# Attention with mixed heads: v's products on 128 rows and half the columns of the array

## The chip, the cores and the metric

The kernel runs on one core of one Trainium2 chip. The metric is the device time of one execution in microseconds (us). The engines are TensorE (in the profile PE for matmuls, PEld for its weight loads), VectorE (DVE), ScalarE (ACT), GpSimd (POOL) and SyncE (SP, which here only issues transfers). Three timed runs of the kernel before gave 973.60, 975.28 and 977.43 us; the median is 975.28 us.

## The reference

Four batches, 12 heads, 448 positions, 64 numbers per head. The scores of all heads are mixed by a 12 x 12 matrix before the softmax, and its result by another one after it. What comes out goes through two dense layers with a leaky rectifier between them.

```python
scores = scale * np.matmul(q, k.transpose(0, 1, 3, 2))
scores = np.einsum('bhij,hg->bgij', scores, w_pre)
attn = np.exp(scores - np.max(scores, axis=-1, keepdims=True))
attn = attn / (np.sum(attn, axis=-1, keepdims=True) + 1e-09)
attn = np.einsum('bhij,hg->bgij', attn, w_post)
attn_out = np.matmul(attn, v)
x = attn_out.transpose(0, 2, 1, 3).reshape(B * S, H * D)      # 1792 x 768
h = x @ w_in                                                  # 768 x 2048
g = np.maximum(h, 0.0) + alpha * np.minimum(h, 0.0)
return g @ w_out                                              # 2048 x 768
```

The arrays w_in, w_out and alpha arrive as 64-bit floats and are rounded in the kernel.

## The kernel before, in words

The work has two phases. The first is the attention, the second the two dense layers (L430 to L530), which read the attention's output back from device memory (`x2`).

Phase one takes queries in 16 chunks: four per batch, with 120, 120, 120 and 97 queries (`CHUNKS`; the last one is used from its row 7 on, 90 queries). A chunk's scores are made head pair by head pair (`qk`, L146), copied by ScalarE to `st` (L154) and sent by DMA into another layout (`relay`, L163), in which 10 queries by 12 heads lie on the partitions. A group is ten queries; two groups make a block, and there are 90 blocks. For each block `mix` (L171) multiplies by w_pre, VectorE takes the row maximum (`rmax`, L176), ScalarE the exponential and its sum (`exp`, L183), VectorE scales w_post by the sums (`norm`, L189 to L193), and `post` (L205) multiplies by that, which also turns the block so that keys lie on the partitions. `post_out` (L215) copies the result into `at`, a tile of [128, 4, 12, 120]: the 448 keys are four blocks of 128, where the last one holds 64, in heads and queries.

`pv` (L217 to L235) multiplies `at` of a whole chunk by `v`, in two halves that stand in two neighbouring steps. Its output `x` takes two banks of PSUM, with three pairs of heads in each. Each product uses a quarter of TensorE's array, 64 rows by 64 columns: 64 keys of one head. Rows 0 to 63 hold the even blocks of 64 keys, rows 64 to 127 the odd ones; the two heads of a pair lie on the two column halves. While rows 0 to 63 add into one bank, rows 64 to 127 add into the other, and in the second half of `pv` the banks are exchanged (`bank = r ^ half`), so that in the end both banks have all keys. The last block of 64 odd keys does not exist, so the lower rows do 24 products of a half and the upper ones 18: 42 in all.

The program never lets both row halves add into one bank at one time: between the halves of `pv` VectorE copies one column of `at` onto itself (L401 to L405): the copy comes after the first half, which reads that tile, and the second half waits for it. `pv_out` (L237) copies both banks to `xe` after the second half.

`step(m)` (L381) writes out the order of the work by hand. On TensorE it is: `mix` of block m+1, `post` of block m-2, and then up to two places for other work, `(m, 0)` and `(m, 1)`; the table `places` puts a `qk` head pair or a half of `pv` into each. The first half of `pv` stands at the second place of a step, the second half at the first place of the next. VectorE also does the rounding of w_in and w_out in between (`convert`, L52 to L58), SP loads q, k, v and those weights, GpSimd issues the relays.

`v` comes from a pool of two buffers, a new tile for each batch (L131 to L134).

Of the kernel before, what the change touches and what calls it, by code (L numbers as in the profile page):

```python
# [8 lines left out]
F32 = mybir.dt.float32  # L9
# [10 lines left out]
B, H, S, D = 4, 12, 448, 64  # L20
DM, DFF = 768, 2048
# [7 lines left out]
CW = 120  # L29
# [3 lines left out]
NS = 4  # L33
NJ = S // 64
# [27 lines left out]
def talking_heads_prelu(ctx: ExitStack, tc: tile.TileContext, q, k, v, w_pre, w_post, mask, w_in, w_out, alpha, out):  # L62
    nc = tc.nc
# [23 lines left out]
    pool = lambda name, bufs, **kw: p1.enter_context(tc.tile_pool(name=name, bufs=bufs, **kw))  # L87
# [6 lines left out]
    sm = pool("sm", 4)  # L94
    ep = pool("ep", LAG + 2)
    rp = pool("rp", LAG + 1)
    vp = pool("vp", 2)
    ap_ = pool("ap", 2)
    xep = pool("xep", 2)
    ps_m = pool("ps_m", 2, space=PSUM)  # L100
# [6 lines left out]
    wq = mixw.tile([128, H, HI], F32, name="wq")  # L107
    NSR = 2 * (RAHEAD + 1)
    sr_b = [srp.tile([128, S], F32, tag=f"sr{i}", name=f"sr{i}") for i in range(NSR)]
    pa = ps_a.tile([128, 2, 512], F32, tag="a", name="pa")  # L110


    k_t, q_t, v_t, s_t, a_t = {}, {}, {}, {}, {}
# [14 lines left out]
                               in_=q[b, :, H * c0 + NP * hf * cn:H * c0 + NP * (hf + 1) * cn])  # L128

    def load_v(b, s):  # L130
        if s == 0:  # L131
            v_t[b] = vp.tile([128, NS, DM], F32, tag="v", name=f"v{b}")
        n = min(128, S - 128 * s)
        nc.sync.dma_start(out=v_t[b][:n, s, :], in_=v[b, 128 * s:128 * s + n])  # L134

# [29 lines left out]
    def mix(m):  # L165

        ps = ps_m.tile([128, 2, 512], F32, tag="m", name=f"m{m}")
        ga, gb = sr_t.pop(2 * m), sr_t.pop(2 * m + 1)
        for hf, g in ((0, ga), (64, gb)):
            for u, r in ((0, slice(0, 64)), (1, slice(64, SR0 + GP))):  # L170
                nc.tensor.matmul(ps[hf:hf + 64, u, :S], wk[r, :], g[r, :], start=True, stop=True)  # L171
        m_t[m] = ps

    def rmax(m):
        nm = sm.tile([128, 2], F32, tag="nm", name=f"nm{m}")
        nc.vector.tensor_reduce(out=nm, in_=m_t[m][:, :, :S], axis=AX.X, op=ALU.max, negate=True)  # L176
        nm_t[m] = nm
# [39 lines left out]
    def pv(ci, half):  # L217


        b, c = chunk_list[ci]  # L220
        cn = ROWS[c][1] * GI
        if half == 0:
            u_t["pv", ci] = ps_s.tile([128, 2, 512], F32, tag="s", name=f"x{ci}")
        ps = u_t["pv", ci]
        for cl in range(3):
            for s in range(NS):
                for r in range(2 if 2 * s + 1 < NJ else 1):
                    bank = r ^ half
                    pr = slice(64 * r, 64 * r + 64)
                    for t in range(2):  # L230
                        h = 2 * (3 * bank + cl) + t
                        nc.tensor.matmul(ps[64 * t:64 * t + 64, bank, cl * CW:cl * CW + cn],  # L232
                                         v_t[b][pr, s, h * D:(h + 1) * D], a_t[ci][pr, s, h, :cn],
                                         start=(half == 0 and s == 0 and cl == 0),
                                         stop=(half == 1 and 2 * s + 2 + r >= NJ and cl == 2))  # L235

    def pv_out(ci, half):  # L237

# [51 lines left out]
    places = {}  # L290
    for ci in range(NC):
        m = (first[ci + 1] - 1) // 2 + LAG + 1
# [21 lines left out]
    with tc.manual_schedule():  # L314
        p0 = ExitStack()
        start = p0.enter_context(tc.tile_pool(name="start", bufs=1))
# [20 lines left out]
        for t in sr_b:  # L337
            nc.vector.memset(t[:SR0], 0.0)
        nc.vector.memset(pa, 0.0)
        for i, w in enumerate((w_pre, w_post)):  # L340
            for p in ((SR0, 64), (0, 64))[i]:
                nc.gpsimd.dma_start(out=mask_sb[p:p + HP, i], in_=mask[:HP, :HI, :])
                nc.gpsimd.dma_start(out=wb[p:p + HP, i, :],
                                    in_=w.rearrange("(o h) g -> o h g", o=1).to_broadcast([HI, H, H]))
# [36 lines left out]
        def step(m):  # L381


            nonlocal done
            for f, *args in jobs.get(m, []):
                f(*args)
            if live(m + 1):
                mix(m + 1)
            now, later[:] = list(later), []
            for f in now:  # L390
                f()
            if live(m - LAG):
                post(m - LAG)
            if live(m - 1):
                norm(m - 1)
            if live(m + 1):
                rmax(m + 1)
            if live(m):
                exp(m, 0)
            use((m - 1, 1), 1)  # L400
            if places.get((m, 0), " ")[0] == "pv":  # L401


                col = a_t[places[m, 0][1]][:, :, :, 0]
                nc.vector.tensor_copy(col, col)  # L405
            if m >= 0:
                relays(2 * (m + 2 + RAHEAD) if m > 2 else first[1], (nc.gpsimd,))
            if live(m):
                exp(m, 1)
            use((m, 0), 0)  # L410
            if live(m - LAG):
                post_out(m - LAG)
            use((m, 0), 1)
            use((m, 1), 0)
            want = (m + 1) * conv_steps // (NB - 4)
            while done < want and done < conv_steps:
                next(conv, None)
                done += 1
# [95 lines left out]
        for u in range(NU + 1):  # L514
            b, f = divmod(u, NFC)
# [4 lines left out]
            if u < NU:  # L520
                split_w(u, 1)
                ps = l1(u)
# [44 lines left out]
```

## Time and profile before

| | |
|---|---|
| median of three runs | 975.28 us |
| the profiled execution | 971.61 us, of which the span of instructions is 969.8 us |
| TensorE matmul | 827.7 us busy (85%), 11540 instructions |
| TensorE weight load | 671.6 us (69%), 11540 instructions |
| VectorE | 488.0 us (50%), 870 instructions |
| ScalarE | 441.5 us (46%), 870 instructions |
| mean granted clock of TensorE | 0.963 of 2.4 GHz |

A written matmul on 32-bit floats appears as two matmul records and two weight loads. A row of the timeline merges neighbours of one kind: start, length from the first start to the last end, engine, line, operation, tiles, shape, number, and in brackets the idle time before them and what ended it. "issue" stands where the profile knows nothing that the engine waited for. `64*64` in a TensorE row is the used part of the array (rows by columns), `64x120` the moving operand. PEclk is the granted share of 2.4 GHz.

### The profile page before, as it was taken

The numbers are of one execution on the slowest core, as the hardware profiler recorded it, in microseconds if no ns is written. First come the engines' busy times: TensorE is split into PE (matmuls) and PEld (weight loads), VectorE is DVE, ScalarE is ACT, GpSimd is POOL, SyncE is SP. The second block draws the span as 40 slices with busy tenths as digits, with TensorE's granted clock in tenths as the row PEclk, the third lists the DMA queues.
The fourth block names the chain that finished last, engine by engine and source line by source line (L and its number), as shares of the span: only waits on it lengthen the run. The fifth ranks groups of instructions, "written<-read, shape, count | busy, mean of one in ns | idle before, by whom it ended". The sixth has DMA issues, their size and how long they took to land.

```text
span 969.8 us, 26257 instructions
## 1 busy us (share of the span) xinstructions
PE 827.7 (85%) x11540; PEld 671.6 (69%) x11540; DVE 488.0 (50%) x870; ACT 441.5 (46%) x870; POOL 353.7 (36%) x315
## 2 busy tenths in 40 slices
PE   6757767777777786787759999999999999999998
PEld 3335544444555453455649999999999999999997
DVE  3756666655766775678252246432454225532222
ACT  1756756665656785677422233333223223233222
POOL 2312222221222221222035545545545545545542
PEclk9989999998989999999879999999999999999999
DMA  6996798765887867775088000200002000010001
GB/s 166 245 255 190 207 267 214 207 186 186 230 248 209 244 207 217 216 217 172 20 305 337 1 10 10 95 1 1 18 2 95 1 1 20 1 57 1 1 1 57
DMA packets 55166, 124.03 MB, mean 128 GB/s; under 512 B 26028, under 2 KB 32988, under 8 KB 55052
## 3 DMA queue, kind: packets, MB, share of 16 engines
q1 hardware_dynamic: 39846, 81.71, 27.7%
q0 software_dynamic: 14208, 37.56, 14.1%
q10 hardware_dynamic: 998, 3.09, 1.0%
q8 instruction: 90, 1.47, 0.6%
q14 instruction: 24, 0.20, 0.1%
HBM read 59.96 MB, written 23.62 MB: 86 GB/s over the span
## 4 chain that ended last, share of the span: by engine, by line
PE 68%; issue 15%; ACT 6%; DMA 5%; POOL 3%; DVE 3%; ACTq 0%; SPq 0%; POOLq 0%; DVEq 0%
PE h L471 24%; PE acc L496 24%; PE x L232 6%; PE pa L205 5%; PE m L171 4%; PE s L146 4%; ACT at L215 3%; ACT st L154 3%; POOL sr L163 2%; DMA sr<-st 2%; DMA v<-in_v_dram 1%; DVE nm L176 1%; DMA xr<-x 1%; DMA wb<-in_w_post_dram 1%; ACT e L183 0%
## 5 line engine op out<-in xcount | busy, mean ns | idle before, releaser
L471 PE MATMUL h<-xs,wi 128*128 128x448 f32 x1152 | 246.4, 368 | 12.7 <-DVE xs L461 11.4
L496 PE MATMUL acc<-g,wo 128*128 128x448 f32 x1152 | 243.7, 365 | 0.0
L471 PEld LDWEIGHTS h<-xs,wi 128*128 128x128 f32 x1152 | 218.1, 189 | 30.7 <-issue 11.5
L163 POOL DMA_DIRECT2D sr<-st x174 | 107.0, 617 | 339.4 <-PE m L171 245.3
L496 PEld LDWEIGHTS acc<-g,wo 128*128 128x128 f32 x1152 | 216.4, 188 | 17.0
L449 POOL TENSOR_TENSOR wi<-wr,wi 128x768 fp32r<-128x768 f32 x64 | 118.6, 1854 | 256.5 <-ACT wi L448 256.5
L176 DVE TENSOR_REDUCE nm<-m 128x2 f32<-128x896 f32 x90 | 98.1, 1089 | 137.1 <-PE m L171 137.1
L480 DVE TENSOR_SCALAR t<-h,alpha_sb 128x448 f32<-128x448 f32 x64 | 43.8, 684 | 236.0 <-PE h L471 236.0
L482 ACT CAST g<-t 128x448 fp32r<-128x448 f32 x64 | 36.3, 567 | 271.3 <-DVE t L481 271.3
L205 PEld LDWEIGHTS pa<-r,e 64*64 64x64 f32 x5040 | 110.4, 139 | 71.0 <-issue 47.5
L146 PE MATMUL s<-k,q 64*64 64x448 f32 (+2 forms) x768 | 103.6, 594 | 55.3 <-ACT st L154 49.9
L205 PE MATMUL pa<-r,e 64*64 64x60 f32 x5040 | 111.5, 226 | 28.2 <-issue 24.1
L215 ACT COPY at<-pa 128x480 f32<-128x480 f32 x180 | 93.1, 572 | 81.6 <-PE pa L205 77.3
L449 POOL TENSOR_TENSOR wo<-wr,wo 128x768 fp32r<-128x768 f32 x64 | 125.2, 1956 | 5.4 <-ACT wo L448 5.4
L183 ACT ACTIVATE e<-m,nm 128x448 f32<-128x448 f32 x180 | 115.2, 646 | 5.4 <-DVE nm L176 3.5
L232 PE MATMUL x<-at,v 64*64 64x120 f32 (+1 forms) x2688 | 91.7, 275 | 26.0 <-issue 16.8
L171 PE MATMUL m<-sr,wk 64*64 64x448 f32 (+1 forms) x720 | 97.3, 575 | 14.8 <-issue 9.1
L154 ACT COPY st<-s 120x896 f32<-120x896 f32 (+1 forms) x93 | 84.9, 913 | 45.1 <-PE s L146 44.9
L232 PEld LDWEIGHTS x<-at,v 64*64 64x64 f32 x2688 | 82.7, 141 | 31.6 <-issue 18.5
L146 PEld LDWEIGHTS s<-k,q 64*64 64x64 f32 (+2 forms) x768 | 23.9, 134 | 98.3 <-ACT st L154 86.4
L448 ACT CAST wo<-wr 128x768 fp32r<-128x768 f32 x64 | 53.5, 836 | 57.2 <-PE acc L496 57.2
L483 DVE TENSOR_TENSOR g<-t,g 128x448 fp32r<-128x448 f32 x64 | 40.8, 638 | 44.6 <-ACT g L482 44.6
(40 smaller groups left out, 489.1 us busy)
## 6 DMA issues: line engine op xcount, KB each, us to landing
sr<-st POOLq DMA_DIRECT2D x174, 210.0 KB, 6.0
cr<-in_w_in_dram SPq DMA_DIRECT2D x16, 768.0 KB, 7.2
cr<-in_w_out_dram SPq DMA_DIRECT2D x16, 768.0 KB, 6.9
wsc<-ct SPq DMA_DIRECT2D x32, 384.0 KB, 6.4
wr<-wsc SPq DMA_DIRECT2D x14, 768.0 KB, 9.9
xr<-x SPq DMA_DIRECT2D x24, 224.0 KB, 3.8
out_dram<-o SPq DMA_DIRECT2D x24, 224.0 KB, 2.0
k<-in_k_dram SPq DMA_DIRECT2D x21, 224.0 KB, 5.9
```

The lines of the kernel that those rows point to most:

```text
L146: nc.tensor.matmul(ps[lo:hi, hf, :S], q_t[ci][r, p, lo:hi], k_t[b][r, p, :], start=True, stop=True)
L154: copy(dst[:cn, p], u_t.pop(("qk", ci, p))[:cn, :, :S])
L163: dma.dma_start(out=sr_t[n][SR0:SR0 + GP], in_=s_t[ci][r0:r0 + (GI - 1) * st + 1:st])
L171: nc.tensor.matmul(ps[hf:hf + 64, u, :S], wk[r, :], g[r, :], start=True, stop=True)
L176: nc.vector.tensor_reduce(out=nm, in_=m_t[m][:, :, :S], axis=AX.X, op=ALU.max, negate=True)
L183: nc.scalar.activation(out=e_t[m][:, u], in_=m_t[m][:, u, :S], func=AF.Exp, bias=nm_t[m][:, u:u + 1], scale=1.0, accum_out=se_t[m][:, u:u ...
L205: nc.tensor.matmul(dst[:, :, HI * u:HI * u + HI], e[h, u, 64 * jb:64 * jb + 64], r[h, u].rearrange("p (h i) -> p h i", h=H), start=True, s ...
L215: nc.scalar.copy(dst, pa[:, g, :NS * GP].rearrange("p (s i) -> p s i", i=GI))
L232: nc.tensor.matmul(ps[64 * t:64 * t + 64, bank, cl * CW:cl * CW + cn], v_t[b][pr, s, h * D:(h + 1) * D], a_t[ci][pr, s, h, :cn], start=(ha ...
L449: nc.gpsimd.tensor_tensor(t[:, 1], w, t[:, 0], ALU.subtract)
L471: nc.tensor.matmul(ps[:, :S], w[:, tw, cc * 128:(cc + 1) * 128], x[:, tx, cc, :], start=(i == 0), stop=(i == 3 * NCC - 1))
L496: nc.tensor.matmul(accs[c][:, :S], w[:, tw, c * 128:(c + 1) * 128], g[:, tg], start=(f == 0 and i == 0), stop=(f == NFC - 1 and i == 2))
```

## The change

`pv` now uses all 128 rows and half the columns for one product: 128 keys of one head. A half of `pv` does the three head pairs of one bank completely (24 products, the two heads of a pair on the two column halves) and the other half those of the other bank. No bank is exchanged, and the copy on VectorE between the halves is gone. Since the fourth block has only 64 keys, rows 64 to 127 of that block are filled with zeros: the two buffers of `v` are made once, with a name each, are zeroed there at the start, and the loads of v write the first 64 rows only.

```diff
@@ -94,7 +94,7 @@
     sm = pool("sm", 4)
     ep = pool("ep", LAG + 2)
     rp = pool("rp", LAG + 1)
-    vp = pool("vp", 2)
+    vp = pool("vp", 1)
     ap_ = pool("ap", 2)
     xep = pool("xep", 2)
     ps_m = pool("ps_m", 2, space=PSUM)
@@ -107,6 +107,7 @@
     wq = mixw.tile([128, H, HI], F32, name="wq")
     NSR = 2 * (RAHEAD + 1)
     sr_b = [srp.tile([128, S], F32, tag=f"sr{i}", name=f"sr{i}") for i in range(NSR)]
+    v_b = [vp.tile([128, NS, DM], F32, tag=f"v{i}", name=f"v{i}") for i in range(2)]
     pa = ps_a.tile([128, 2, 512], F32, tag="a", name="pa")
@@ -128,8 +129,7 @@
                                in_=q[b, :, H * c0 + NP * hf * cn:H * c0 + NP * (hf + 1) * cn])
     def load_v(b, s):
-        if s == 0:
-            v_t[b] = vp.tile([128, NS, DM], F32, tag="v", name=f"v{b}")
+        v_t[b] = v_b[b % 2]
         n = min(128, S - 128 * s)
         nc.sync.dma_start(out=v_t[b][:n, s, :], in_=v[b, 128 * s:128 * s + n])
@@ -224,15 +224,10 @@
         ps = u_t["pv", ci]
         for cl in range(3):
             for s in range(NS):
-                for r in range(2 if 2 * s + 1 < NJ else 1):
-                    bank = r ^ half
-                    pr = slice(64 * r, 64 * r + 64)
-                    for t in range(2):
-                        h = 2 * (3 * bank + cl) + t
-                        nc.tensor.matmul(ps[64 * t:64 * t + 64, bank, cl * CW:cl * CW + cn],
-                                         v_t[b][pr, s, h * D:(h + 1) * D], a_t[ci][pr, s, h, :cn],
-                                         start=(half == 0 and s == 0 and cl == 0),
-                                         stop=(half == 1 and 2 * s + 2 + r >= NJ and cl == 2))
+                for t in range(2):
+                    h = 2 * (3 * half + cl) + t
+                    nc.tensor.matmul(ps[64 * t:64 * t + 64, half, cl * CW:cl * CW + cn], v_t[b][:, s, h * D:(h + 1) * D],
+                                     a_t[ci][:, s, h, :cn], start=(s == 0), stop=(s == NS - 1))
     def pv_out(ci, half):
@@ -337,6 +332,8 @@
         for t in sr_b:
             nc.vector.memset(t[:SR0], 0.0)
         nc.vector.memset(pa, 0.0)
+        for t in v_b:
+            nc.vector.memset(t[S % 128:, NS - 1, :], 0.0)
         for i, w in enumerate((w_pre, w_post)):
             for p in ((SR0, 64), (0, 64))[i]:
                 nc.gpsimd.dma_start(out=mask_sb[p:p + HP, i], in_=mask[:HP, :HI, :])
@@ -398,11 +395,6 @@
             if live(m):
                 exp(m, 0)
             use((m - 1, 1), 1)
-            if places.get((m, 0), " ")[0] == "pv":
-                col = a_t[places[m, 0][1]][:, :, :, 0]
-                nc.vector.tensor_copy(col, col)
             if m >= 0:
                 relays(2 * (m + 2 + RAHEAD) if m > 2 else first[1], (nc.gpsimd,))
             if live(m):
```

On TensorE, the two steps in which the first chunk's `pv` stands, before. The names are those of the program with its running numbers; `m` is the output of `mix`, `pa` of `post`, `x` of `pv`. "x41" says that the row stands for 41 such instructions as written, and brackets name the engines or DMA queues that the instruction waits for.

```order
L205 MATMUL pa_118<-r6_669,e6_608 64x12x5 x27
L232 MATMUL x0_733<-at0_369,v0_252 64x120 [waits DMAHW1_49,PE_49]
L232 MATMUL x0_733<-at0_369,v0_252 64x120 x3
...
L232 MATMUL x0_733<-at0_369,v0_252 64x120 [waits DMAHW7_49]
L232 MATMUL x0_733<-at0_369,v0_252 64x120 x29
L171 MATMUL m10_785<-sr4_114,wk_108 64x448 [waits DMASW7_49,DVE_49,Activation_49]
...
L205 MATMUL pa_118<-r7_720,e7_673 64x12x5 x27
L232 MATMUL x0_733<-at0_369,v0_252 64x120 [waits DVE_49]
L232 MATMUL x0_733<-at0_369,v0_252 64x120 x41
L171 MATMUL m11_883<-sr6_116,wk_108 64x448 [waits DMASW1_49,PE_49,Activation_49]
```

And the same place now:

```order
L205 MATMUL pa_120<-r6_672,e6_611 64x12x5 x27
L229 MATMUL x0_736<-at0_372,v0_118 64x120 [waits DMAHW1_49,PE_49]
L229 MATMUL x0_736<-at0_372,v0_118 64x120
...
L229 MATMUL x0_736<-at0_372,v0_118 64x120 [waits DMAHW7_49]
L229 MATMUL x0_736<-at0_372,v0_118 64x120 x17
L171 MATMUL m10_770<-sr4_114,wk_108 64x448 [waits DMASW7_49,DVE_49,Activation_49]
...
L205 MATMUL pa_120<-r7_723,e7_676 64x12x5 x27
L229 MATMUL x0_736<-at0_372,v0_118 64x120 x24
L171 MATMUL m11_849<-sr6_116,wk_108 64x448 [waits DMASW1_49,DVE_49,Activation_49]
```

A half goes from 42 to 24 written products, nothing around it moves, and the second half has no wait of its own any more.

On VectorE, before, between the row maximum of block 10 and the rounding steps (`ct`, `ce`) of the same program step:

```order
L193 TENSOR_TENSOR r8_822<-wq_109,s18_819 128x120 [waits DVE_49]
L176 TENSOR_REDUCE nm10_824<-m10_785 128x2 [waits PE_49]
L405 COPY at0_369<-at0_369 128x48
L54 TENSOR_SCALAR ce1_1_779<-ce1_1_779 128x768
L55 SCALAR_TENSOR_TENSOR ct1_1_780<-cr1_1_562,ct1_1_780 128x768
```

And now:

```order
L193 TENSOR_TENSOR r8_807<-wq_109,s18_804 128x120 [waits DVE_49]
L176 TENSOR_REDUCE nm10_809<-m10_770 128x2 [waits PE_49]
L54 TENSOR_SCALAR ce1_1_764<-ce1_1_764 128x768
L55 SCALAR_TENSOR_TENSOR ct1_1_765<-cr1_1_565,ct1_1_765 128x768
```

The copy stood behind the row maximum, which itself waits for `mix` on TensorE; the rest keeps its order.

## Rows read from the trace of the kernel before

**Rows 1.** The page: the span, the busy time of each engine with its share and instructions, and of the DMA queues the one whose packets are instructions (packets, MB, share of 16 engines).

```profile
span 969.8 us, 26257 instructions
...
PE 827.7 (85%) x11540; PEld 671.6 (69%) x11540; DVE 488.0 (50%) x870; ACT 441.5 (46%) x870; POOL 353.7 (36%) x315
...
q8 instruction: 90, 1.47, 0.6%
```

**Rows 2.** Windows over the two phases: from and to, length, then busy us and instructions of PE, PEld, DVE, ACT and POOL, the granted clock, the share of time in which the DMA engines are busy, and GB/s.

```profile
0.00:481.50 481.50, 355.90 (x9156) 235.22 (x9160) 303.92 (x618) 298.47 (x664) 112.51 (x187) 0.94 0.74 206
485.00:969.80 484.80, 469.81 (x2304) 434.57 (x2304) 184.09 (x252) 142.39 (x204) 241.19 (x128) 0.99 0.14 51
```

**Rows 3.** The waits of TensorE's matmuls, by line and by what ended them: total us, times, longest us.

```profile
PE s L146 <- ACT st L154: 49.9, 44, 1.5
...
PE pa L205 <- issue: 24.1, 12, 5.2
...
PE x L232 <- issue: 16.8, 9, 3.7
...
PE m L171 <- issue: 9.1, 3, 3.8
...
PE x L232 <- DVE at L405: 4.6, 9, 0.9
```

**Rows 4.** The timeline of TensorE in two neighbouring steps with two `qk` each: the start of the first `qk` of a step.

```profile
88.32 0.97 PE L146 MATMUL s<-k,q 64*64 64x448 f32 x8 [1.17 <-ACT st L154]
...
92.90 0.97 PE L146 MATMUL s<-k,q 64*64 64x448 f32 x8 [1.17 <-ACT st L154]
```

**Rows 5.** The timeline of TensorE around the two halves of `pv` of one chunk.

```profile
126.88 2.52 PE L232 MATMUL x<-at,v 64*64 64x120 f32 x80
...
129.17 0.33 PE L232 MATMUL x<-at,v 64*64 64x120 f32 x2
129.28 0.98 PE L171 MATMUL m<-sr,wk 64*64 64x448 f32 x6
...
133.73 0.27 PE L205 MATMUL pa<-r,e 64*64 64x60 f32 x2 [2.61 <-issue]
...
133.90 2.46 PE L232 MATMUL x<-at,v 64*64 64x120 f32 x79
...
136.91 0.89 PE L205 MATMUL pa<-r,e 64*64 64x60 f32 x32
140.99 0.27 PE L205 MATMUL pa<-r,e 64*64 64x60 f32 x2 [3.20 <-issue]
```

**Rows 6.** Windows, each from a restart of TensorE after an "issue" wait to the next one; columns as in rows 2.

```profile
133.73:140.99 7.26, 4.06 (x127) 3.73 (x128) 3.39 (x10) 3.10 (x8) 1.46 (x2) 1.00 1.01 274
159.20:165.86 6.66, 3.41 (x128) 2.98 (x127) 5.36 (x12) 2.95 (x8) 1.46 (x2) 1.00 0.99 198
189.19:197.30 8.11, 3.96 (x128) 3.42 (x128) 3.15 (x7) 1.03 (x2) 1.15 (x2) 1.00 1.04 253
366.50:373.49 6.99, 4.02 (x128) 3.24 (x127) 1.76 (x5) 3.09 (x8) 0.57 (x1) 1.00 0.81 209
```

**Rows 7.** The DMA view of two short stretches, 130.9 to 132.3 us and 138.6 to 139.8 us, both within a stop of TensorE: the queue of instructions.

```profile
q8 instruction: 1, 0.02, 5.9%
...
q8 instruction: 1, 0.02, 5.8%
```

**Rows 8.** From the chain of waits in the second phase, one piece (start, us, what), and the page's group of these matmuls (busy us, mean ns | idle before).

```profile
506.33 3.65 PE acc L496 x18
...
L496 PE MATMUL acc<-g,wo 128*128 128x448 f32 x1152 | 243.7, 365 | 0.0
```

**Rows 9.** The groups by form: v's products, chunks of 120 and of 90 queries.

```profile
L232 PE MATMUL x<-at,v 64*64 64x120 f32 x2016 | 72.6, 282 | 19.3 <-issue 12.9 <-ACT st L154 3.5 <-DVE at L405 2.9
...
L232 PE MATMUL x<-at,v 64*64 64x90 f32 x672 | 19.1, 256 | 6.7 <-issue 3.9 <-DVE at L405 1.7 <-ACT at L215 1.1
```

**Rows 10.** The view of the tile `x`: number and shortest, median and longest duration in ns, first and last start.

```profile
L232 PEld LDWEIGHTS x<-at,v x2688: 129/133/228, 65.6 to 483.2; 64*64 64x64 f32 x192
L232 PE MATMUL x<-at,v x2688: 237/263/459, 65.6 to 483.2; 64*64 64x120 f32 x144, 64*64 64x90 f32 x48
```

**Rows 11.** A window behind the stop at 140.99 us (columns as in rows 2), and the timeline of TensorE: `mix` in it, and `mix` a step later.

```profile
143.10:146.50 3.40, 2.99 (x16) 1.00 (x20) 0.00 (x0) 2.13 (x5) 0.00 (x0) 0.50 0.77 243
...
145.06 1.63 PE L171 MATMUL m<-sr,wk 64*64 64x448 f32 x8
...
150.35 0.93 PE L171 MATMUL m<-sr,wk 64*64 64x448 f32 x8
```

**Rows 12.** The timeline of TensorE at the start, where matmuls on 128*128 follow `qk` on 64*64.

```profile
16.48 1.28 PE L328 MATMUL warm<-warm 128*128 128x448 f32 x5
```

**Rows 13.** VectorE: the row maximum, the copy, one memset (groups: busy us, mean ns | idle before), and the wait of L349 (total us, times, longest).

```profile
L176 DVE TENSOR_REDUCE nm<-m 128x2 f32<-128x896 f32 x90 | 98.1, 1089 | 137.1 <-PE m L171 137.1
...
L405 DVE COPY at<-at 128x48 f32<-128x48 f32 x16 | 3.3, 209 | 13.0 <-PE x L232 13.0
...
L339 DVE MEMSET pa<- 128x1024 f32 x1 | 0.9, 912 | 0.2 <-issue 0.2
...
DVE wk L349 <- DMA wb<-in_w_pre_dram: 5.5, 1, 5.5
```

## The prediction

> **What bounds the kernel now.** I read the windows by phase first [rows 1, 2]. From 485 us on TensorE has 469.8 of 484.8 us busy in 2304 matmuls at 0.99 of its clock: that phase holds none of the changed code, and I leave it as it is. Before it, 355.9 of 481.5 us are busy, the DMA engines move data for 0.74 of the time, and the clock is 0.94. All of the change lies there.
>
> Next the waits of TensorE [rows 3]. Two kinds matter. 49.9 us in 44 waits stand before `qk`, for ScalarE to empty the one score buffer; they belong to the score steps, which come every 4.58 us (88.32 to 92.90) [rows 4] and which the change does not touch. 50.0 us (24.1 + 16.8 + 9.1) in 24 waits are named "issue": TensorE waits for nothing that the profile knows.
>
> The timeline shows where these stand [rows 5]: in the steps with v's products. TensorE runs from 126.88 without a break, stops, goes on at 133.73 after 2.61 us, works, and goes on again at 140.99 after 3.20 us. The windows from one such restart to the next [rows 6] hold 127 or 128 matmuls and 127 or 128 weight loads each: 256 instructions, four times over, with round trips of 7.26, 6.66, 8.11 and 6.99 us, mean 7.26. The page gives queue q8, kind "instruction", 90 packets and 1.47 MB [rows 1]; TensorE has 2 x 11540 instructions, which is 256 per packet. And in each of the two stops just one q8 packet moves [rows 7]. So TensorE stops when its next 256 instructions have not come; their packet queues with data on DMA engines that are 0.81 to 1.04 busy there [rows 6]. In the last phase 18 matmuls take 3.65 us, 0.203 each [rows 8], so 256 instructions last 26 us and the packet is always early.
>
> The Trainium skill, "Runtime: NRT & Kernel Launch", section "Instruction fetch mechanics", names blocks of 256 instructions and calls the cost of crossing into one mostly hidden. By that the removal of instructions would be worth nothing; the trace agrees on the 256 and shows 50.0 us that are not hidden.
>
> **The change, part by part.**
>
> *Fewer instructions.* A half of `pv` has 84 matmul records and as many loads, 2016 + 672 = 2688 in 32 halves [rows 9]. Each written matmul gives two records. After the change a half has 24 written matmuls, 48 records and 48 loads: 96 instructions in place of 168. A step with one half (16 for `mix`, 112 for `post`) goes from 296 to 224. In all 32 x 72 = 2304 instructions go, 9 of the 90 packets.
>
> *How long a half takes.* At present 80 of 84 matmuls take 2.52 us to the end of the last [rows 5]. The two tiles of rows 0 to 63 have 24 passes each, those of rows 64 to 127 have 18. Over 24 passes that is at most 0.105 us a pass; I use 0.103 (2.47 us a half). After the change there are again 24 passes of 120 columns in each column half. If the halves run side by side, as two column tiles on the same 64 rows must do now (one after the other they would need 48 x 0.103 = 4.9 us), a half still takes 2.5 us. The trace has no tile of 128 rows and 64 columns: from below I allow 2.3 us (without the uneven row groups), from above 4.9 us. I take 2.5 us, since 64*64 with the same columns and moving width is the nearest row.
>
> *The instruction waits.* In the four windows TensorE is busy 4.06, 3.41, 3.96 and 4.02 us, mean 3.86, before it waits the other 3.40. With 224 instructions in a step, 256 of them hold 296/224 as much work: 5.10 us. With the same round trip each wait shrinks by 1.24 us. 24 equal waits of 2.08 us would leave 20 us; they are not equal (the longest is 5.2) and the short ones can't go below zero, so I put what is left at 24 us. The dense steps also fill fewer packets: 32 x 296/256 = 37 before, 28 now, which scales 24 to 18. I take 21 between the two, a gain of **29 us**. Bounds: 0, if the packets come later by what the work is longer, and 50.
>
> *The copy on VectorE.* L405 goes, 16 times, and with it the second half's wait for it: 4.6 us in 9 waits [rows 3]. The copy stands behind the row maximum, 1.09 us on VectorE [rows 13], so this is a real gap on TensorE, not covered by the packet waits, which stand elsewhere. Gain **4.6 us** (0 to 4.6). The second half then has no wait of its own; VectorE's own order loses 0.21 us per copy, which nobody waits for otherwise.
>
> *The clock.* 0.94 over 481.5 us is 29 us of lost clock, 58 us at 1.2 GHz. In one such stretch, granted 0.50, right behind the stop at 140.99, `mix` takes 1.63 us where a step later it takes 0.93 [rows 11]. Fewer and shorter stops should leave fewer of these stretches. Some stand at the start, for other reasons, and in score steps ScalarE sets the pace. I take **4 us** (0 to 12).
>
> *The array's other shape.* `post`, `mix` and `qk` stay on 64*64, `pv` does not: 64 changes of shape, in and out of 32 halves. The trace has one such place, from 64*64 to 128*128 at 16.48 [rows 12]: five matmuls take 1.28 us, while 5 x 0.203 plus the last one's tail (0.365 - 0.203 [rows 8]) is 1.18, so 0.10 us is lost in filling. A drained array shows in full the tail of the last matmul, 0.263 - 0.103 = 0.16 us [rows 10]. Together 0.26 at most, 0 at least; I take 0.2 us: **+12.8 us** (0 to 17). It is not hidden, since TensorE is the bound in these steps. The early start of `mix` beside the last of `pv` (129.28, while `pv` ends at 129.50) [rows 5] is given up within it.
>
> The Trainium skill, "TensorEngine Tiling (Array Packing)", section "Key Properties", says that a change of tiling mode drains TensorE. It gives no time; the one place here fits it, and without a drain the sum would be lower by the 12.8 us.
>
> *Zeros and buffers.* Two memsets of 64x768 on VectorE: 1024 columns took 0.91 us, so about 0.7 each by the columns. They stand before L349, which waits 5.5 us for a DMA [rows 13], and are hidden; uncovered, 1.4 us. v's loads keep their places on SP's queue and their sizes, and two buffers take turns as before: 0.
>
> Sum: -29 - 4.6 - 4 + 12.8 = -24.8. On the profiled execution's 971.6 this gives 946.8. That execution lies 3.7 under the median of 975.3, so the forecast in terms of medians is **950 us**.
>
> **Rivals.**
>
> *The shape changes cost more.* If each takes 0.5 us, twice what I can read from one place, they cost 32 us, and the waits shrink by some 4 more as the steps grow: 975 - 29 - 4 - 4.6 - 4 + 32 = 965; at 0.7 us each, 978. For it: there is one place only, and it stands behind another wait. Against it: 0.10 and 0.16 are all that the rows show.
>
> *The packets come later still.* Their delay is that of queues shared with the relays and loads. If requests shift with the longer work, the waits stay at 45: -5 - 4.6 + 12.8 gives 978. Against it: the windows with 3.41 us of work have no longer round trip than those with 4.06 [rows 6].
>
> *Column halves do not run side by side on full rows.* A half then takes 4.9 us: +2.47 for 24 halves, +1.85 for the 8 of 90 columns, 74 us. The instruction waits almost vanish under it (256 instructions then hold some 7.6 us of work, more than a round trip): -45, with -4.6, -6 and +12.8 the sum is +31: 1006 us. It decides from about 0.8 us more per half on (24.8/32). For it: no such tile in the trace. Against it: two column tiles on the same rows keep one pass in 0.103 us each.
>
> The same end, by another way, is that weights for the same rows no longer load behind the running matmul: a load is 0.129 us at least [rows 10], 24 of them +3.1 us a half, 99 us; with -45, -4.6, -6 and +12.8 the sum is +56: 1031 us. The rows speak against it: 24 passes with 0.103 + 0.129 each would be 5.6 us where 2.5 are measured. The Trainium skill, "TensorE: Matmul & The Clock Gate", section "The mechanism", states this as a rule (loads overlap only where the row group differs); it would give that time, and the trace disagrees, as do the 128*128 matmuls at 0.203 us apiece.
>
> **How the numbers follow.** Forecast 0.62, its own range 936 to 966. Dearer shapes 0.13, late packets 0.11, halves in series 0.10, loads exposed 0.04. Within 0.5% means 970.4 to 980.2, about what a measurement here can tell from no change. Faster: the forecast and 0.05 of the dear shapes, 0.67. Within: 0.05 of the dear shapes and 0.08 of the late packets, 0.13. Slower: 0.03 of each of these and the last two, 0.20. The range, 934 to 985, leaves out the last two cases and a little at either end.
>
> **What would show it.** Right: `x` in 1536 matmuls of 128*64, 81 or 82 q8 packets, "issue" waits on TensorE near 21 us, 48 matmuls of a half in 2.5 us, none named after L405, phase 2 unchanged. Wrong: a half over 3.3 us, "issue" waits still above 40, or gaps of 0.5 us at each side of `pv`.

## The result, and the profile after

The changed kernel takes 945.82 us (median of four executions, 943.48 to 948.94), beside 974.62 for the kernel before (973.6 to 977.43). The ratio is 0.9714 with an interval of [0.9667, 0.9761]. The forecast was 950 us. Ratios leave out slow, disturbed executions, and where the profile fell on one (the experiment with equal parts, and the one with the copy in the whole kernel) only times are given.

The page of the changed kernel: the span, the busy time of each engine, and the queue of instructions, as in [rows 1].

```profile
span 941.7 us, 23967 instructions
...
PE 821.3 (87%) x10388; PEld 662.4 (70%) x10388; DVE 486.7 (52%) x856; ACT 441.3 (47%) x870; POOL 355.6 (38%) x315
...
q8 instruction: 82, 1.34, 0.6%
```

TensorE executes 1152 matmuls and 1152 weight loads fewer, 2304 instructions in all, and the queue brings 82 packets in place of 90. Here are two windows over the phases, with the columns of [rows 2], and three windows from one restart of TensorE to the next, as in [rows 6]:

```profile
0.00:453.00 453.00, 349.46 (x8050) 226.07 (x8052) 302.67 (x604) 298.18 (x664) 114.30 (x187) 0.97 0.80 219
457.00:941.70 484.70, 470.34 (x2304) 434.98 (x2304) 184.04 (x252) 142.42 (x204) 241.32 (x128) 0.98 0.14 51
351.92:359.47 7.55, 5.08 (x127) 2.62 (x127) 4.29 (x11) 5.02 (x10) 0.58 (x1) 1.00 1.03 302
182.34:190.11 7.77, 6.56 (x128) 5.76 (x128) 1.57 (x3) 3.10 (x8) 1.34 (x2) 0.78 0.95 249
385.31:393.18 7.87, 5.44 (x127) 2.71 (x126) 6.07 (x13) 6.26 (x14) 2.85 (x5) 1.00 0.70 209
```

The second phase is as long as before (484.7 against 484.8 us), and the whole gain lies in the first: the last product with v starts at 454.3 us, where it started at 483.2 [rows 10], 28.9 us earlier. The three round trips of 256 instructions take 7.55 to 7.87 us; in all nine of the trace in which one packet separates two neighbouring stops they take 5.3 to 10.1 us. TensorE's waits, by line and by what ended them (total us, times, longest), as in [rows 3]:

```profile
PE s L146 <- ACT st L154: 49.6, 44, 1.3
PE pa L205 <- issue: 25.8, 15, 3.8
...
PE x L229 <- issue: 2.3, 2, 1.2
...
PE s L146 <- issue: 1.3, 1, 1.3
```

The wait for ScalarE before `qk` is what it was. The "issue" waits are 29.4 us in 18 (25.8 + 2.3 + 1.3), where there were 50.0 in 24. Each of the 18 ends 1.2 to 1.6 us after a packet of the instruction queue has moved, as do the 24 before. The wait for the copy is gone, and no wait stands before the second half in its place. The view of the tile `x` (ns shortest, median, longest; first and last start in us), and TensorE's timeline over one chunk's two halves:

```profile
L229 PEld LDWEIGHTS x<-at,v x1536: 132/137/231, 63.8 to 454.2; 128*64 128x64 f32 x192
L229 PE MATMUL x<-at,v x1536: 238/266/460, 63.8 to 454.3; 128*64 128x120 f32 x144, 128*64 128x90 f32 x48
```

```profile
97.81 2.68 PE L229 MATMUL x<-at,v 128*64 128x120 f32 x48 [1.18 <-ACT st L154]
100.42 0.98 PE L171 MATMUL m<-sr,wk 64*64 64x448 f32 x8
...
102.25 2.68 PE L229 MATMUL x<-at,v 128*64 128x120 f32 x48
```

A half has 48 records and takes 2.68 us to the end of its last one; before, 80 of its 84 records took 2.52 [rows 5]. So the two column halves do run side by side on full rows, and the loads, 0.137 us each, lie behind the products: the 24 loads of one column half alone would be 3.3 us. `mix` no longer starts beside the last products, but 2.61 us after the first one.

### The profile page after: what moved, and what is told of

Its sections match the earlier page's. It is cut to its first block, busy times and chain, and to the rows that moved or that the text cites. A ratio compares the mean times of both kernels' runs of the same rounds, so it can differ in the third digit from the quotient of the medians.

```text
span 941.7 us, 23967 instructions
## 1 busy us (share of the span) xinstructions
PE 821.3 (87%) x10388; PEld 662.4 (70%) x10388; DVE 486.7 (52%) x856; ACT 441.3 (47%) x870; POOL 355.6 (38%) x315
## 3 DMA queue, kind: packets, MB, share of 16 engines
q0 software_dynamic: 14208, 37.56, 14.7%
## 4 chain that ended last, share of the span: by engine, by line
PE 66%; issue 15%; ACT 7%; POOL 4%; DMA 3%; DVE 3%; ACTq 0%; POOLq 0%; SPq 0%; DVEq 0%
PE h L463 25%; PE acc L488 25%; PE x L229 5%; PE pa L205 4%; POOL sr L163 4%; PE s L146 4%; PE m L171 3%; ACT st L154 3%; ACT at L215 2%; DMA sr<-st 2%; ACT e L183 1%; DVE nm L176 1%; DMA xr<-x 1%; DMA wb<-in_w_post_dram 1%; DVE ct L58 0%
## 5 line engine op out<-in xcount | busy, mean ns | idle before, releaser
L463 PE MATMUL h<-xs,wi 128*128 128x448 f32 x1152 | 247.0, 368 | 12.9 <-DVE xs L453 11.5
L205 PEld LDWEIGHTS pa<-r,e 64*64 64x64 f32 x5040 | 100.4, 135 | 77.6 <-issue 56.8
L146 PE MATMUL s<-k,q 64*64 64x448 f32 (+2 forms) x768 | 98.9, 561 | 57.2 <-ACT st L154 49.6
L205 PE MATMUL pa<-r,e 64*64 64x60 f32 x5040 | 104.6, 221 | 30.3 <-issue 25.8
L171 PE MATMUL m<-sr,wk 64*64 64x448 f32 x720 | 89.0, 558 | 7.6 <-DMA sr<-st 5.4
L229 PE MATMUL x<-at,v 128*64 128x120 f32 (+1 forms) x1536 | 88.3, 275 | 7.1 <-ACT st L154 3.5
L229 PEld LDWEIGHTS x<-at,v 128*64 128x64 f32 x1536 | 81.3, 146 | 11.7 <-ACT st L154 5.8
## 6 DMA issues: line engine op xcount, KB each, us to landing
k<-in_k_dram SPq DMA_DIRECT2D x21, 224.0 KB, 11.5
```

Of the source, the lines that this page charges most:

```text
L146: nc.tensor.matmul(ps[lo:hi, hf, :S], q_t[ci][r, p, lo:hi], k_t[b][r, p, :], start=True, stop=True)
L205: nc.tensor.matmul(dst[:, :, HI * u:HI * u + HI], e[h, u, 64 * jb:64 * jb + 64], r[h, u].rearrange("p (h i) -> p h i", h=H), start=True, s ...
L229: nc.tensor.matmul(ps[64 * t:64 * t + 64, half, cl * CW:cl * CW + cn], v_t[b][:, s, h * D:(h + 1) * D], a_t[ci][:, s, h, :cn], start=(s == ...
L463: nc.tensor.matmul(ps[:, :S], w[:, tw, cc * 128:(cc + 1) * 128], x[:, tx, cc, :], start=(i == 0), stop=(i == 3 * NCC - 1))
```

## The experiments

**The changed kernel again, and with the instructions put back.** The same kernel was run again on another chip, beside one in which most products are written in two parts along the queries, so that `pv` has as many instructions as before the change.

> The changed kernel once more, on the chip of the three kernels below, as their measure. 0.971 of the kernel before, within its interval 0.967 to 0.976; issue waits on TensorE near 29 us.

> The changed kernel with 18 more written products in a half on the average: four or five of the six chains of a half run over two column parts of half the width. The shape of the array, the sums and the work stay; the 2304 instructions that the change removed are back, 91 packets on the instruction queue. Theory (TensorE waits for its instructions): issue waits on TensorE rise from 29 to 40 to 50 us; the narrower passes cost 7.5 us (58 ns for 60 columns against 51.5, 2 passes, 9 products in each column half, 32 halves); time 18 to 28 us over the changed kernel. Rival (the gain comes from the other shape and the missing wait on VectorE, the instructions are worth nothing): issue waits stay near 29, time 7.5 us over the changed kernel.

```diff
-            for s in range(NS):
-                for t in range(2):
+            for k in range(2):
+                for s in range(NS):
+                    for t in range(2):
+                        two = cl < 2 or half == 1 and t == 0
+                        if k and not two:
+                            continue
+                        lo, hi = ((0, cn // 2), (cn // 2, cn))[k] if two else (0, cn)
...
```

The changed kernel again: 949.18 us, ratio 0.9768 [0.9708, 0.9829], just outside the interval expected. With the instructions back: 977.37 us, 1.0036 [0.9993, 1.0079]. The whole gain is gone. TensorE's waits, of the first and then of the second:

```profile
PE pa L205 <- issue: 21.5, 12, 4.7
PE x L229 <- issue: 7.6, 3, 3.5
...
PE s L146 <- issue: 0.2, 1, 0.2
```

```profile
PE x L234 <- issue: 17.6, 9, 3.2
PE pa L205 <- issue: 17.3, 11, 4.4
```

TensorE's timeline in the second, two halves of one chunk:

```profile
128.43 2.91 PE L234 MATMUL x<-at,v 128*64 128x60 f32 x80
...
134.28 3.02 PE L234 MATMUL x<-at,v 128*64 128x60 f32 x88
```

The "issue" waits rise only from 29.3 to 34.9 us, where 40 to 50 were expected. The halves themselves grow from 2.68 to 2.91 and 3.02 us, (0.23 + 0.34) x 16 = 9 us. The last product starts 21.8 us later (478.0 against 456.2); 14.7 us of that are these two, and the other 7 are not explained. So this experiment shows that the instructions cost time, but not how much of it is their fetching.

**The same, with equal parts.** Two of three head pairs are in two parts in each half (2048 instructions more than the changed kernel); the difference shown is against the kernel just above.

> The changed kernel with the four chains of the first two head pairs of a half in two column parts each, in both halves alike, so that the column halves stay in step: 160 instructions in a half, 2048 of the 2304 are back. The work of a half grows by 0.21 us, as the first halves of the kernel with 18 more products showed (2.63 against 2.42): 6.7 us. Theory (the instructions count): issue waits 35 to 45 us, time 12 to 22 us over the changed kernel. Rival (they do not): issue waits near 29, 6.7 us over it.

```diff
-                        two = cl < 2 or half == 1 and t == 0
+                        two = cl < 2
```

973.6 us, ratio 1.0093 [1.0055, 1.013]. Again the gain is gone, and again work and fetching can't be told apart in it.

**All products on 64 rows.** To take the changes of shape away, `pv` used rows 0 to 63 only, which leaves out half of the keys.

> The changed kernel with pv on rows 0 to 63 alone, which leaves out half of the keys: as many instructions and passes, but every matmul of phase one on 64*64, so no change of shape. Theory (0.14 to 0.15 us lost at each of 64 changes of shape): 9 us faster than the changed kernel, less 1 to 3 that the instruction waits grow, since the steps are shorter. Rival A (changes of shape are free): no difference. Rival B (each costs 0.5 us): 25 to 32 us faster.

```diff
-... v_t[b][:, s, h * D:(h + 1) * D], a_t[ci][:, s, h, :cn], ...
+... v_t[b][:64, s, h * D:(h + 1) * D], a_t[ci][:64, s, h, :cn], ...
```

949.83 us, ratio 0.9797 [0.9726, 0.9868], not faster than the changed kernel (949.18 on the same chip). The first phase's window shows why that settles nothing:

```profile
0.00:463.60 463.60, 361.86 (x8084) 245.41 (x8084) 302.80 (x604) 298.12 (x665) 114.80 (x187) 0.93 0.77 214
```

The granted clock is 0.93, where it was 0.97 and 0.96 in the changed kernel's two traces: 7% of 463.6 us are 32 us of lost clock, in place of 14 and 18. Whatever the missing changes of shape gave back is hidden under that. The price of one half on 64 rows can be read all the same, from an undisturbed one:

```profile
327.14 0.31 PE L229 MATMUL x<-at,v 64*64 64x120 f32 x1
...
327.25 2.63 PE L229 MATMUL x<-at,v 64*64 64x120 f32 x47
```

From 327.14 to 329.88 these are 2.74 us, against 2.68 on 128 rows: the number of rows hardly matters to the products themselves.

**Each bank copied out as soon as it is complete.** Now that a half completes a bank, `pv_out` can copy bank 0 after the first half.

> The changed kernel with the copy of the first bank of x to xe moved ahead by a step, since a half now finishes its bank: one copy instead of two stands between the second half and the next qk. Theory: the 2.8 us that qk waits for xe shrink to about 1.4, the wait of the instructions is untouched, 1 to 3 us faster than the changed kernel, which is within what three rounds can tell. Rival: ScalarE's second exponential of that step comes 0.46 us later and holds up post: 0 to 5 us slower.

```diff
     def pv_out(ci, half):
-        if half == 0:
-            return
...
-        for bank in range(2):
...
+        xe, ps = xe_t[ci], u_t["pv", ci]
+        src = ps[:, half, :3 * CW].rearrange("p (c i) -> p c i", c=3)[:, :, :cn]
...
```

944.49 us, ratio 0.9731 [0.9675, 0.9787]; its interval and those of the changed kernel cover each other. The wait that it was to shorten did become shorter, by 1.1 us from 2.8 (1.4 was expected), but `pv` now waits 0.5 us for this copy once:

```profile
PE s L146 <- ACT xe L242: 1.7, 3, 0.6
```

**The kernel before, once more.** One execution on another chip, for a second trace of its waits.

> The kernel before, profiled once more: how much the sum of its issue waits varies between executions. Theory: 45 to 55 us again, in 20 to 26 waits. If it lies near 30, the 50.0 us on which the sum was built were one unlucky execution.

```profile
PE pa L205 <- issue: 22.8, 11, 3.2
PE x L232 <- issue: 14.6, 9, 3.1
PE m L171 <- issue: 8.9, 3, 4.6
PE x L232 <- DVE at L405: 4.7, 9, 1.1
```

46.3 us of "issue" waits and 4.7 for the copy, as in [rows 3]: the waits on which the sum rests are no accident of one execution. Its last product with v starts at 478.3 us, 22.1 us after that of the changed kernel's second trace (456.2).

**Both kernels without the weights' traffic.** The loads of w_in and w_out in phase one stop after two row blocks, one rounded block is stored, and phase two reads that one for all. The output has wrong weights; the work of every engine but the DMA queues stays.

> The kernel before without the traffic of the weights in phase one: 30 of 32 loads of raw weights and 30 of 32 stores of rounded ones are left out, the rounding runs on the first two again and again, and the second phase reads the first pair for all (so the output is not the reference's). 35 of some 99 MB of phase one go. Theory (instruction packets queue behind data): issue waits fall from 50 to under 20 us, and the time by at least as much, 25 to 45 us. Rival (their round trip is fixed and has nothing to do with data): issue waits stay near 50.

> The changed kernel with the same traffic left out. Theory: issue waits under 10 us; with the packets in time, what is left between the two kernels is the wait for the copy (4.6 us for the changed kernel), the changes of shape (9 us against it) and what remains of the issue waits, so the changed kernel is between 10 us faster and 5 us slower than the one before with the same cut. Rival (the gain comes from the shape or the missing copy): still 20 to 29 us faster.

> The changed kernel without the weights' traffic once more (the loads of two of the row blocks of the weights are used for all, one rounded block is stored and read for all, so w_in and w_out are wrong), as the base of the next two on their chip. Expected: the last product with v near 422 us as the first time (420 to 427), TensorE's issue waits near 9 us, and in an undisturbed half of pv 48 records in 2.42 us. If the place of the end of phase one moves by more than 5 us between two executions of one kernel, differences of this size between kernels say nothing, and only the steps do.

```diff
-            if i < len(todo):
+            if i < 2:
...
-            raw = raw_c.pop(i)
+            raw = raw_c[i % 2]
...
-                later.append(lambda f=f, x=x, t=t: store_c(f, x, t))
+                if f == 0:
+                    later.append(lambda f=f, x=x, t=t: store_c(f, x, t))
...
-            dma.dma_start(out=wr_t[f], in_=wsc[f])
+            dma.dma_start(out=wr_t[f], in_=wsc[0])
```

The kernel before falls to 924.2 us, ratio 0.9531 [0.9422, 0.964]. The changed one takes 911.29 us, 0.9443 [0.9364, 0.9523], and on another chip 913.76 us, 0.942 [0.9336, 0.9505]. The two kernels' intervals overlap, so the times alone don't tell them apart. TensorE's waits and the window of the first phase, of the kernel before:

```profile
PE pa L205 <- issue: 8.2, 7, 2.3
PE x L232 <- DVE at L406: 7.0, 14, 1.2
...
PE x L232 <- issue: 1.9, 2, 1.6
```

```profile
0.00:434.40 434.40, 341.74 (x9236) 227.35 (x9236) 304.05 (x618) 297.50 (x664) 112.06 (x187) 0.97 0.55 148
```

And of the changed kernel (the second execution):

```profile
PE pa L205 <- issue: 5.5, 5, 2.5
...
PE m L171 <- issue: 1.7, 1, 1.7
PE s L146 <- issue: 0.6, 1, 0.6
```

```profile
0.00:423.50 423.50, 340.73 (x8084) 219.28 (x8084) 303.10 (x604) 297.75 (x664) 115.04 (x187) 0.98 0.56 152
```

With the same instructions, and DMA engines busy for 0.55 in place of 0.74 of the time, the "issue" waits of the kernel before shrink from 46 or 50 to 10.1 us, those of the changed one from 29 to 7.8 (9.3 in its first execution). So it is mostly the weights' transfers that make the packets of instructions late. Whether a packet waits for them in the DMA engines or at the memory no run here separates. The Trainium skill, "Runtime: NRT & Kernel Launch", section "Instruction fetch mechanics", calls the crossing mostly hidden: these traces agree, 10 of 434 us, and those with the full traffic do not.

Between the two kernels 10.9 us of phase one remain (the last product starts at 434.2 and 423.3; at 422.2 in the changed kernel's first execution), though their waits for packets differ by 2.3 us only. The clock has a part in this. Here are two short windows of the kernel before, and the whole stretch of the changed kernel from its first product with v to its last:

```profile
168.80:172.20 3.40, 3.03 (x86) 2.98 (x86) 3.21 (x4) 2.57 (x8) 1.15 (x2) 0.51 0.40 143
428.30:431.70 3.40, 3.32 (x80) 3.33 (x82) 0.00 (x0) 0.02 (x1) 0.00 (x0) 0.50 0.02 5
```

```profile
66.30:423.30 357.00, 296.10 (x7452) 197.70 (x7448) 265.59 (x531) 265.60 (x602) 96.18 (x153) 1.00 0.50 142
```

In its two short windows the kernel before has the lower clock, 1.2 GHz, which costs at most half of 6.8 us; the changed kernel has none. So 5 to 9 us of the difference are neither late packets nor clock. With the traffic as quiet, the other parts can be seen alone.

**The copy put back.** The changed kernel without the weights' traffic, with the copy that nothing needs any more.

> The changed kernel without the weights' traffic (as above), and with the copy of one column of `at` between the halves of pv put back, which nothing needs now. Theory (the copy costs more than the idle time that the trace names after it, since TensorE also drains and fills again): 0.65 to 0.8 us in each of 16 places, phase one longer by 10 to 13 us than without the copy. Rival (the copy costs what its named waits are, 4.6 us in 9 waits, as forecast): phase one longer by 4 to 6 us. Third: the second half waits for nothing, because a step's mix and post are long enough: 0 to 1 us.

```diff
             use((m - 1, 1), 1)
+            if places.get((m, 0), " ")[0] == "pv":
+                col = a_t[places[m, 0][1]][:, :, :, 0]
+                nc.vector.tensor_copy(col, col)
```

TensorE's timeline over the same chunk, first without and then with the copy:

```profile
119.99 2.68 PE L229 MATMUL x<-at,v 128*64 128x120 f32 x48
...
123.40 1.10 PE L205 MATMUL pa<-r,e 64*64 64x60 f32 x56
124.43 2.68 PE L229 MATMUL x<-at,v 128*64 128x120 f32 x48
```

```profile
122.63 2.68 PE L229 MATMUL x<-at,v 128*64 128x120 f32 x48
...
126.04 1.09 PE L205 MATMUL pa<-r,e 64*64 64x60 f32 x56
127.58 2.68 PE L229 MATMUL x<-at,v 128*64 128x120 f32 x48 [0.44 <-DVE at L401]
```

The second half starts 1.03 us after `post` without the copy and 1.54 with it: 0.51 us. Ten of the 14 such places show just this step; the other four show 0.53 to 0.98. The last product starts at 430.7 us, 7.4 later. That is above the forecast's 4.6 and below the 10 to 13 expected here; both sizes were wrong, and 0.51 x 16 = 8.2 us is what I take. The waits that the trace names for it are 7.1 us here. By whole times the two can't be told apart (915.99 us, ratio 0.9427 [0.9342, 0.9512]); one reason is in the last section.

**More changes of shape.** The changed kernel without the weights' traffic, with the middle head pair of each half on rows 0 to 63 (half of its keys are left out): as many instructions, two changes of shape more per half.

> The changed kernel without the weights' traffic (as above), with the middle one of the three head pairs of each half of pv on rows 0 to 63 alone (half of the keys are left out there): as many instructions, two changes of shape more in each half, 64 in all, 128*64 to 64*64 and back. Theory (a change of shape costs 0.145 us by itself): a half takes 2.71 us in place of 2.42, phase one 9 us longer. Forecast's size, 0.2 us each: 2.82 us and 13 us longer. Rival (the loss at the edges of pv is that of other operands or another bank, not of the shape): 2.42 us and no difference.

```diff
-... v_t[b][:, s, h * D:(h + 1) * D], a_t[ci][:, s, h, :cn], ...
+... v_t[b][:64 if cl == 1 else 128, s, h * D:(h + 1) * D], a_t[ci][:64 if cl == 1 else 128, s, h, :cn], ...
```

The same chunk on the timeline, and the end of the phase:

```profile
121.98 2.98 PE L229 MATMUL x<-at,v 128*64 128x120 f32 x48
...
430.56 7.61 PE L229 MATMUL x<-at,v 128*64 128x90 f32 x96 [1.13 <-ACT at L215]
```

A half takes 2.98 us in place of 2.68: 0.30 for two changes, 0.15 each. It is the change and not the 64 rows that costs: a whole half on 64 rows, without a change, took 2.74 us. The Trainium skill, "TensorEngine Tiling (Array Packing)", section "Key Properties", says that such a change drains TensorE; the loss here agrees with that. The ratio is 0.9566 [0.9484, 0.9648], 927.6 us. The last product starts 14.6 us later than without the extra changes, more than the 9.6 of 64 changes: the last 96 matmul records took 7.61 us in place of 3.94, with a granted clock of 0.85 in the last 23 us in place of 1.00.

**The copy put back in the whole kernel.** The same three lines of the copy in the changed kernel.

> The changed kernel whole, with the copy of one column of `at` on VectorE between the halves of pv put back, which nothing needs now. Theory (0.65 to 0.8 us in each of 16 places, less where a wait for instructions covers it): the gain of 28 us falls to 16 to 20, ratio to before 0.979 to 0.984. Rival (4.6 us as forecast): ratio 0.974 to 0.977, not to be told from the changed kernel.

954.71 us as the median of all four; the two that the ratio is taken from took 943.73 and 948.85 us, which gives 0.9746 [0.963, 0.9862]. The interval covers what either side expected; the run decides nothing.

## Why the prediction was right, and which of its terms were not

The path was as forecast: phase two stays, halves keep their time, TensorE waits less for instructions, the copy's wait goes, and changes of shape take part of it back. None of the rivals came. Column halves in series or exposed loads would show as halves of 4.9 us or more; 2.68 are there. Waits that stay at 45 us did not come (29.4 and 29.3). Changes of shape at 0.5 us each did not either (0.15). The sum held in part by luck: errors of its terms stood against each other. In us, for the pair of first traces and for the second pair (the kernel before once more, and the changed one again):

| term | forecast | first pair | second pair |
|---|---|---|---|
| instruction waits | -29 | -20.6 (50.0 to 29.4) | -17.0 (46.3 to 29.3) |
| copy (quiet kernels: 16 x 0.51) | -4.6 | -4.6 to -8.2 | -4.6 to -8.2 |
| changes of shape, 16 x 0.15 to 0.3 | +12.8 | +2.4 to +4.8 | +2.4 to +4.8 |
| the rest, clock among it | -4 | -2.5 to -8.5 | +0.7 to -5.3 |
| phase one, last product | -24.8 | -28.9 | -22.1 |

The first row and the last are read from the traces of each pair. The copy and the changes of shape are taken from the quiet kernels, and the rest is what is left.

*Instruction waits: too large by 8 to 12 us.* The step that failed is "with the same round trip each wait shrinks by 1.24 us", together with the choice of 21 us. In the three windows above the round trip is 7.55 to 7.87 us, a little longer than the mean of 7.26 [rows 6], and the waits that end them are 1.1 to 1.3 us: there the rule erred on the safe side, since it gave 2.16. But over the whole phase 18 waits remain with a mean of 1.63 us and up to 3.8, where there were 24 with 2.08; in the second pair 16 with 1.83, where there were 23 with 2.01. So a wait shrank by 0.45 and 0.18 us, not by 1.24, and the larger part of the gain is that there are fewer of them, 18 in place of 24 in the first pair. Of the prediction's two scalings the one by packets, 28 in place of 37, came close to that count. A packet's delay is no constant; the runs without the weights' traffic show that it depends on that traffic. In the changed kernel the same data moves in a shorter phase (DMA engines busy 0.80 of the time in place of 0.74), which may be why the trips didn't get shorter; no run tests it. Why single packets are later than others in the same kernel was not settled.

*The copy: too small.* I took the 4.6 us that the trace names, 9 waits of 16. Put back alone, the copy costs 0.51 us at the places where nothing else is late. In the kernel before, the quiet run names 14 waits with 7.0 us: with full traffic, part of these lie under waits for instructions. The two terms overlap, then: 8.2 us is what the copy is worth once the packets come in time, and with the full traffic it lies between the 4.6 named and that. No run here measures it there.

*Changes of shape: sized fairly, counted too often.* 0.15 us each against my 0.2. But not all 64 show on the path. In the quiet kernels, the three steps from one row maximum to the third after it, around one chunk's `pv`, take 13.61 us before, 13.39 in the changed kernel and 13.89 with the copy put back. VectorE's timeline, the first and the last of these row maxima, in this order of kernels:

```profile
120.45 1.08 DVE L176 TENSOR_REDUCE nm<-m 128x2 f32<-128x896 f32 x1
...
134.06 1.09 DVE L176 TENSOR_REDUCE nm<-m 128x2 f32<-128x896 f32 x1 [2.22 <-PE m L171]
```

```profile
119.43 1.08 DVE L176 TENSOR_REDUCE nm<-m 128x2 f32<-128x896 f32 x1
...
132.82 1.09 DVE L176 TENSOR_REDUCE nm<-m 128x2 f32<-128x896 f32 x1 [2.06 <-PE m L171]
```

```profile
122.08 1.08 DVE L176 TENSOR_REDUCE nm<-m 128x2 f32<-128x896 f32 x1
...
135.97 1.09 DVE L176 TENSOR_REDUCE nm<-m 128x2 f32<-128x896 f32 x1 [2.07 <-PE m L171]
```

So the whole new layout without the copy's gain costs 13.89 - 13.61 = 0.28, some 0.3 us a chunk, where four changes at 0.15 would be 0.60. Around three other undisturbed chunks it is 0.25 to 0.31, and around four it is 0.15 to 0.17 (in the sixth chunk 16.38 us before, 16.02 changed, 16.54 with the copy). For the part that is hidden the timeline offers two reasons: the second half used to start on an array that had drained anyway while it waited for the copy, and after the second half ScalarE's copies set when the next `qk` starts. Neither was tried by itself.

*The clock.* It rose from 0.94 to 0.97 (second pair 0.94 to 0.96). By that the lost clock fell from 29 to 14 us (second pair 29 to 18), but how much of it lay where TensorE sets the pace is not known. My 4 us lies within what is left for the clock and the start of the phase, 2.5 to 8.5 and -0.7 to 5.3 us; no run shows it by itself. In the quiet pair the terms add up: -2.3 for the waits, 0 to -3.4 for the clock, -8.2 for the copy and 2.4 to 4.8 for the shape give -5.7 to -11.5, where -10.9 was measured.

*The halves and the zeros.* 2.5 us was forecast, and 48 records take 2.42 us from the first start to the last, 2.68 to the end. The memsets at the start cost nothing that can be seen: the first product with v starts at 63.8 us, not later than before (65.6 [rows 10]).

## What to carry to other kernels

Where TensorE stops for "issue" in dense steps of small matmuls while the DMA engines are busy, count its instructions (256 to a packet here) and see what else moves at that time: here taking data out of the queues shortened the waits more than taking 2304 instructions away did. A short wait in the middle of a dense stretch can be worth more than the trace names for it, when a longer wait covers it at some of its places and then goes. And a change of the array's shape, 0.15 us in the middle of a dense stretch here, cost on the path only a quarter to a half of that at the edges of `pv`, so don't count each such change in full.

## What the hardware showed that I had not expected

The second phase has two paces, in the same code, at a granted clock of 1.00 from 520 to 900 us in either: in some executions 18 matmuls take 3.65 us, in others 3.72. From the chain of waits, the changed kernel first and its second execution after:

```profile
485.40 3.65 PE acc L488 x18
```

```profile
505.87 3.72 PE h L463 x18
```

With 2304 / 18 = 128 such pieces that is 9.0 us, most of the 10.9 between the profiled times of the two executions (943.48 and 954.36). The kernel before shows both too (3.65 [rows 8], 3.72 in its second trace), and so do the quiet kernels: in the profiled executions the one with the copy had 3.65 (918.9 us) and the one without it 3.72 (921.63 us), which is why these two times hide the copy. The pace is fixed within an execution, and both occur on one chip. What sets it is open. When a change of 1% is measured on one execution, this must be taken out first, stage by stage.

The other surprise is the clock under half-used rows: the products on rows 0 to 63 alone, with as many instructions and less to multiply, ran in a phase with 0.93 granted in place of 0.96 and 0.97, and the kernel was no faster for it. Over the whole kernel its four executions had 0.953 to 0.962, those of the changed kernel on the same chip 0.967 to 0.974. Why is open.
